# The last output tile cut into 384 and 128 columns, its last part copied and stored by ScalarE

## Chip, cores, metric

One core of one Trainium2 chip. The metric is the device time of one execution in microseconds (us), lower is better.

Names in the profile: PE is TensorE, PEld its weight loads, DVE VectorE, ACT ScalarE, POOL GpSimd, SP SyncE. A "q" after the name is the engine's queue, in which DMAs are issued. L637 is line 637 of the kernel file. A store has "landed" when the last of its 16 completion increments (the counts that its DMA adds to a semaphore) has arrived.

## The reference

Windowed attention with a few global keys (4 batches, 8 heads, 768 positions, head size 64), followed by a feed-forward layer with squared ReLU. Only the last product matters here:

```python
def _moe_ref(x, w_in, w_out):          # x: 3072 x 512, d_ff = 2048
    h = np.maximum(x @ w_in, 0.0)
    return (h * h @ w_out).astype(np.float32)
```

The output is 3072 x 512 in float32, written in 24 tiles of 128 rows. The change concerns the 24th.

## The kernel before

A small planner in Python places operations in an order at build time. An operation is listed with the engines that may do it and their costs. An ordinary output tile is one group of 16 matmuls of 512 columns, one copy out of PSUM and one store of 256 KB. The very last tile has its own function:

```python
    def copy(e, out, in_):
        if e == "ACT":
            nc.scalar.copy(out=out, in_=in_)
        else:
            eng(e).tensor_copy(out=out, in_=in_)
    # ... cut ...
    def last_layer2(x, j):
        n = d_model // 2
        r0 = x.hb * HALF + j * P
        for c in range(0, d_model, n):
            st = {}

            def emit(e, c=c, st=st):
                st["ps"] = bank([P, 512], FP32, "yps")
                for m in range(NFT):                       # NFT = 16
                    nc.tensor.matmul(st["ps"][:, 0:n], lhsT=x.h2[:, m, j * P:(j + 1) * P],
                                     rhs=w_out_sb[:, m, c:c + n], start=m == 0, stop=m == NFT - 1)

            def evac(e, st=st):
                st["y"] = y_p.tile([P, d_model], FP32, name="y", tag="y")
                copy(e, st["y"][:, 0:n], st["ps"][:, 0:n])
            job = plan.pe(NFT * (n / 2400 + 0.003), emit, [x.h2_ops[m, j] for m in range(NFT)], 1)
            y_op = plan.after(job, {"ACT": 0.3, "DVE": 0.35}, evac)
            plan.add({"SP": 0.6}, lambda e, c=c, st=st: nc.sync.dma_start(
                out=out[r0:r0 + P, c:c + n], in_=st["y"][:, 0:n]), [y_op])
    # ... cut ...
        if hb == NHB - 1:
            main = main[:-NFT // 4] + [lambda: last_layer2(x, HT - 1)]
```

So the last tile is already cut in two halves: the copy and the store of the first half go on beside the matmuls of the second.

The softmax here doesn't subtract the row's maximum and nothing guards it: scores larger than these inputs give would overflow.

## Time and profile before

| | before |
|---|---|
| time, median (lowest to highest) | 213.84 us (213.76 to 214.04) |
| span of the profiled execution | 212.0 us |
| TensorE busy | 206.4 us, 97% |
| first matmul of the last tile | 205.22 us |
| last matmul ends | 208.87 us |
| last copy, ScalarE, 256 columns | 208.91 to 209.28 us |
| last store issued, landed | 209.31, 211.0 us |

How to read it: everything up to 208.9 us is bound by TensorE. What can be gained by the change lies in the 3.1 us after it, in which one copy, one store and the closing of the program follow each other with nothing beside them. I call this stretch, from the end of the last matmul to the end of the span, the **tail**. The views that show it stand in the prediction below.

### The profile page before, as it was taken

To read this page: it belongs to the slowest core of one execution; us is meant where nothing else is said; L and a number is where in the kernel's file an instruction comes from. 1 tells how busy PE (TensorE), PEld (TensorE's weight loads), DVE (VectorE), ACT (ScalarE), POOL (GpSimd) and SP (SyncE) were. 2 spreads that over 40 slices of the span, in tenths; PEclk is the share of its full clock that TensorE was granted. 3 is DMA by queue.
4 is the path that set the end of the run, shared out by engine and by line. 5 is a ranking of instruction groups with operands and counts; after the bars stand their busy time and mean duration, and the time that the engine had idled before them with its cause. 6 is when DMAs were issued, how large, how long until landed. Compare 5 with 4: busy or idle time off the path is not lost.

```text
span 212.0 us, 4795 instructions
## 1 busy us (share of the span) xinstructions
PE 206.4 (97%) x1902; PEld 127.6 (60%) x1902; DVE 116.3 (55%) x332; ACT 122.5 (58%) x252; POOL 66.5 (31%) x82
## 2 busy tenths in 40 slices
PE   6999999999999999999999999999999999999994
PEld 7877898755554665456644665456644665455553
DVE  8679878434681678319860778218860777114300
ACT  6899897735741994148811994248811994247421
POOL 8997343594001930094008600095000000000000
PEclk9999999999999999999999999999999999999999
DMA  6999999999954999599988995399941100320012
GB/s 175 167 164 197 199 198 209 163 154 169 179 162 136 118 152 145 136 121 178 142 112 128 168 152 111 91 125 174 153 120 77 53 19 19 90 99 2 0 53 99
DMA packets 106343, 27.06 MB, mean 128 GB/s; under 512 B 96976, under 2 KB 103376, under 8 KB 106320
## 3 DMA queue, kind: packets, MB, share of 16 engines
q0 software_dynamic: 74944, 13.11, 80.0%
q1 hardware_dynamic: 30320, 13.11, 27.4%
q10 hardware_dynamic: 1056, 0.52, 0.8%
q8 instruction: 15, 0.25, 0.5%
q14 instruction: 8, 0.07, 0.1%
HBM read 27.26 MB, written 6.29 MB: 158 GB/s over the span
## 4 chain that ended last, share of the span: by engine, by line
PE 88%; POOL 6%; DMA 5%; DVE 0%; ACT 0%; issue 0%; POOLq 0%
PE hps L560 39%; PE yps L609 38%; DMA w_in_sb<-in_moe_w_in_dram 5%; PE sp L464 4%; PE av L519 4%; POOL v L312 2%; POOL sk L312 2%; POOL sq L312 2%; PE yps L637 2%; PE trp L411 1%; PE av L760 1%; POOL w_in_sb L369 0%; PE trx L787 0%; PE sp L721 0%; DVE ident L239 0%; ACT y L200 0%
## 5 line engine op out<-in xcount | busy, mean ns | idle before, releaser
L560 PE MATMUL hps<-xt,w_in_sb 128*128 128x384 f16 (+2 forms) x608 | 88.0, 301 | 0.1
L609 PE MATMUL yps<-w_out_sb,h 128*128 128x512 f16 x368 | 83.0, 379 | 0.0
L560 PEld LDWEIGHTS <-w_in_sb 128*128 128x128 f16 x608 | 53.9, 98 | 26.9 <-DMA w_in_sb<-in_moe_w_in_dram 0.4
L584 ACT ACTIVATE hr<-hps 128x384 f16<-128x384 f32 (+1 forms) x107 | 55.3, 525 | 13.8 <-PE hps L560 12.0
L609 PEld LDWEIGHTS <-h 128*128 128x128 f16 x368 | 34.9, 98 | 39.0
L200 ACT COPY y<-yps 128x512 f32<-128x512 f32 (+1 forms) x25 | 14.2, 568 | 66.5 <-PE yps L609 56.8
L595 DVE TENSOR_TENSOR h<-hr 128x768 f16<-128x768 f16 (+1 forms) x70 | 35.4, 521 | 24.5 <-ACT hr L584 24.0
L312 POOL DMA_DIRECT2D sq<-in_q_dram x22 | 19.5, 897 | 67.1 <-DMA xt<-tm 63.9
L477 ACT ACTIVATE ex<-sp 128x512 f16<-128x512 f32 x66 | 35.1, 624 | 1.2 <-PE sp L464 1.2
L586 DVE TENSOR_SCALAR hr<-hps 128x384 f16<-128x384 f32 x15 | 8.3, 554 | 38.7 <-PE hps L560 38.7
L312 POOL DMA_DIRECT2D v<-in_v_dram x24 | 21.5, 927 | 4.7 <-DMA w_out_sb<-in_moe_w_out_dram 3.7
L497 DVE TENSOR_TENSOR phat<-ex,mask 128x1024 f16<-128x1024 f16 (+1 forms) x36 | 20.3, 598 | 2.1 <-ACT ex L477 2.1
L312 POOL DMA_DIRECT2D sk<-in_k_dram x22 | 19.5, 910 | 3.4 <-DMA w_out_sb<-in_moe_w_out_dram 2.9
L529 DVE TENSOR_TENSOR tm<-av,rec 128x384 f16<-128x384 f32 x24 | 13.4, 558 | 0.8
L202 DVE COPY vb<-v 128x520 f16<-128x520 f16 (+1 forms) x32 | 10.2, 318 | 3.2 <-DMA v<-in_v_dram 2.7
L519 PEld LDWEIGHTS <-phat 128*128 128x128 f16 x240 | 9.8, 98 | 3.1
L519 PE MATMUL av<-v,phat 128*128 128x65 f16 x144 | 10.9, 194 | 0.0
L519 PE MATMUL av<-vb,phat 128*128 128x65 f16 x96 | 10.1, 194 | 0.0
L464 PEld LDWEIGHTS <-qk 64*128 64x128 f16 x168 | 6.3, 94 | 4.6 <-issue 3.7
L464 PE MATMUL sp<-qk 64*128 64x128 f16 x168 | 8.8, 218 | 0.0
L202 DVE COPY kb<-qk 128x96 f16<-128x96 f16 (+4 forms) x56 | 7.9, 205 | 0.8 <-ACT qk L200 0.4
L527 DVE RECIPROCAL rec<-av 128x6 f32<-128x6 f32 x24 | 4.7, 195 | 6.7 <-PE av L519 6.2
(66 smaller groups left out, 137.8 us busy)
## 6 DMA issues: line engine op xcount, KB each, us to landing
out_dram<-y SPq DMA_DIRECT2D x23, 256.0 KB, 2.2
v<-in_v_dram POOLq DMA_DIRECT2D x24, 128.0 KB, 7.0
sq<-in_q_dram POOLq DMA_DIRECT2D x22, 128.0 KB, 5.7
sk<-in_k_dram POOLq DMA_DIRECT2D x22, 128.0 KB, 6.3
w_in_sb<-in_moe_w_in_dram POOLq DMA_DIRECT2D x4, 512.0 KB, 10.5
w_out_sb<-in_moe_w_out_dram POOLq DMA_DIRECT2D x4, 512.0 KB, 15.7
y<-in_k_dram ACTq DMA_DIRECT2D x2, 256.0 KB, 4.5
y<-in_q_dram SPq DMA_DIRECT2D x2, 256.0 KB, 4.0
```

The costliest lines, as they stand in the source:

```text
L200: nc.scalar.copy(out=out, in_=in_)
L202: eng(e).tensor_copy(out=out, in_=in_)
L312: dma = nc.gpsimd.dma_start(out=dst, in_=src[x.b, :, r0 + t * P:r0 + (t + 1) * P, :] .rearrange("h p d -> p h d"))
L464: nc.tensor.matmul(sp[h][:, i, :], lhsT=lhsT, rhs=bt.qk[rows, 0, r, a, :], start=True, stop=True)
L477: nc.scalar.activation(out=st["ex"][:, h], in_=sp[h], func=AF.Exp, scale=scale)
L497: eng(e).tensor_tensor(out=x.phat[a][:, :, t0:t0 + n], op=ALU.mult, in0=st["ex"][:, :, i0:i0 + 2 * n].rearrange("p e (t b) c -> p e t (b c ...
L519: nc.tensor.matmul(av[:, h, j, :], lhsT=lhsT, rhs=rhs, start=not before, stop=before or r == 0)
L529: nc.vector.tensor_tensor(out=st["tm"].rearrange("p t e d -> p e t d"), in0=av[:, :, :, 0:D], in1=rec[:, :, :, None].to_broadcast([P, 2, H ...
L560: nc.tensor.matmul(st["ps"][:, i * n:(i + 1) * n], lhsT=w_in_sb[:, kk, m * P:(m + 1) * P], rhs=x.xt[:, kk, c0:c1], start=kk == 0, stop=kk ...
L584: nc.scalar.activation(out=o, in_=i, func=AF.Relu)
L595: eng(e).tensor_tensor(out=x.h2[:, m0:m0 + width, c0:c1], in0=hr, in1=hr, op=ALU.mult)
L609: nc.tensor.matmul(st["ps"], lhsT=x.h2[:, m, j * P:(j + 1) * P], rhs=w_out_sb[:, m, :], start=m == 0, stop=m == NFT - 1)
```

## The change

Its intent: a shorter last part (128 columns in place of 256) makes the last copy and the last store shorter. The longer first part is moved out by VectorE, and the last store is issued by ScalarE right behind its own copy, from a queue that holds nothing else.

```diff
-        n = d_model // 2
         r0 = x.hb * HALF + j * P
-        for c in range(0, d_model, n):
+        for c, n in ((0, 384), (384, d_model - 384)):
             st = {}
 ... (n=n, queue=queue handed to the inner functions) ...
-            y_op = plan.after(job, {"ACT": 0.3, "DVE": 0.35}, evac)
-            plan.add({"SP": 0.6}, lambda e, c=c, st=st: nc.sync.dma_start(
+            y_op = plan.after(job, {"DVE" if c == 0 else "ACT": 0.09 + n * 0.001}, evac)
+            q, queue = ("SP", nc.sync) if c == 0 else ("ACT", nc.scalar)
+            plan.add({q: 0.6}, lambda e, c=c, n=n, st=st, queue=queue: queue.dma_start(
                 out=out[r0:r0 + P, c:c + n], in_=st["y"][:, 0:n]), [y_op])
```

More of the change, by code (lines that the diff above doesn't have):

```diff
@@ L628, in last_layer2, with emit @@
     def last_layer2(x, j):
-        n = d_model // 2
         r0 = x.hb * HALF + j * P
-        for c in range(0, d_model, n):
+        for c, n in ((0, 384), (384, d_model - 384)):
             st = {}
-            def emit(e, c=c, st=st):
+            def emit(e, c=c, n=n, st=st):
                 st["ps"] = bank([P, 512], FP32, "yps")
@@ L638, in emit, with evac @@
                                      rhs=w_out_sb[:, m, c:c + n], start=m == 0, stop=m == NFT - 1)
-            def evac(e, st=st):
+            def evac(e, n=n, st=st):
                 st["y"] = y_p.tile([P, d_model], FP32, name="y", tag="y")
```

## The prediction

> **What bounds the kernel now.** I read the busy shares first, then the chain that ended last, then the last seven microseconds in order of time, and last the movement of the final store in quarter microseconds. The page gives a span of 212.0 us and says who is full:
>
> ```profile
> PE 206.4 (97%) x1902; PEld 127.6 (60%) x1902; DVE 116.3 (55%) x332; ACT 122.5 (58%) x252; POOL 66.5 (31%) x82
> ```
>
> TensorE is busy for 97% of the span, so the body is bound by matmuls, and the change does not touch the body. The chain of waits from 195 us on shows where its reach begins:
>
> ```profile
> 198.47 6.91 PE yps L609 x32
> 205.38 3.51 PE yps L637 x32
> 208.89 0.02 issue
> 208.91 0.37 ACT y L200
> ```
>
> Line 637 is the last tile: 32 matmuls of 256 columns, then one copy. Until 208.89 us only matmuls stand on the chain. What follows is an exposed tail of 212.0 - 208.9 = 3.1 us. The timeline of the last stretch, and the source view of the store (for its issue: least, median and largest ns):
>
> ```profile
> 205.22 3.66 PE L637 MATMUL yps<-w_out_sb,h 128*128 128x256 f16 x32
> 205.42 0.59 ACT L200 COPY y<-yps 128x512 f32<-128x512 f32 x1 [2.87 <-PE yps L609]
> 207.16 0.37 ACT L200 COPY y<-yps 128x256 f32<-128x256 f32 x1 [1.16 <-PE yps L637]
> 207.56 2.08 SPq L645 DMA_DIRECT2D out_dram<-y  x2
> 208.91 0.37 ACT L200 COPY y<-yps 128x256 f32<-128x256 f32 x1 [1.38 <-PE yps L637]
> ```
>
> ```profile
> L645 SPq DMA_DIRECT2D out_dram<-y x2: 332/332/332, 207.6 to 209.3; - x2
> DMA to landing us min/median/max: 1.7/1.7/1.7
> ```
>
> The merged store row holds two issues: the first from 207.56, and the last, which ends at 207.56 + 2.08 = 209.64 and so begins at 209.64 - 0.33 = 209.31, some 30 ns after the copy's end at 208.91 + 0.37 = 209.28. It lands at 209.31 + 1.7 = 211.01. The remaining 1.0 us is the closing exchange of semaphores between the engines. The SP queue was idle from 207.89 to 209.31: the second store waited for its copy and not for a busy queue. The window view (length, busy time by engine, then clock, DMA share, GB/s) splits the 1.7 us:
>
> ```profile
> 210.00:210.25 0.25, 0.00 (x0) 0.00 (x0) 0.00 (x0) 0.00 (x0) 0.00 (x0) 1.00 0.34 123
> 210.25:210.50 0.25, 0.00 (x0) 0.00 (x0) 0.00 (x0) 0.00 (x0) 0.00 (x0) 1.00 1.02 361
> 210.50:210.75 0.25, 0.00 (x0) 0.00 (x0) 0.00 (x0) 0.00 (x0) 0.00 (x0) 1.00 0.14 41
> ```
>
> The 16 DMA engines are busy for 0.25 x (0.34 + 1.02 + 0.14) = 0.375 us, from about 210.17 to 210.54. So of the 1.7 us, 0.86 pass from issue to first byte, 0.37 are movement, and 0.47 pass until the completion is seen. The two stores before agree: the one of 207.56 began to move at about 208.42, also 0.86 later, and the 256 KB one of 205.99 moved for 0.68 us and landed in 2.0.
>
> **What the Trainium skill says.** (1) "DMA: Bandwidth & Descriptors", section "Issuing engines are not separate DMA queues": stores issued from ScalarE and from SyncE run on the same 16 DMA engines, and a second issuer only saves sequencer time. The trace gives that saving nothing to take here, the SP queue being idle for 1.4 us. (2) "ScalarE: Activation LUTs", section "What ACT_TABLE_LOAD costs": 0.833 ns per element. The trace agrees: copies of 512 and of 256 columns take 585 and 372 ns, (585 - 372)/256 = 0.832. (3) "TensorE: Matmul & The Clock Gate", section "Back-to-back issue gap": alone N/2.4 + 2.5 ns, but about 81 ns for N = 128 in a stream with weight loads. The 256-column tile agrees with the first form: (3.66 - 0.272)/31 = 109 ns, against 109.2. At 128 columns the trace contradicts the 81 ns, as shown below.
>
> **The change part by part.** In the built instruction streams the two kernels differ only in this last tile: matmuls of 16 x 384 and 16 x 128 columns for 32 x 256, one copy on VectorE and one on ScalarE for two on ScalarE, one store on each queue for two on SP. Nothing earlier moves.
>
> TensorE. Columns and instruction count are unchanged, 16 x 512 and 32. The rates come from a 128-column group in the opening, one of 16 back to back, and from layer 1 near the end of the chain, 64 matmuls of 384 columns:
>
> ```profile
> 19.31 1.06 PE L560 MATMUL hps<-xt,w_in_sb 128*128 128x128 f16 x16
> ```
>
> ```profile
> 188.07 10.40 PE hps L560 x64
> ```
>
> At 128 columns a single matmul shows 219 ns, so the gap is (1.06 - 0.219)/15 = 56 ns; at 384 it is 10.40/64 = 162.5 ns. From 205.22: 16 x 0.1625 = 2.60, the first part's last result at 205.22 + 15 x 0.1625 + 0.326 = 207.98 (326 ns is the mean of 384-column matmuls late in the trace), and the end at 205.22 + 2.60 + 15 x 0.056 + 0.219 = 208.88. Before: 205.22 + 3.66 = 208.88. Gain zero.
>
> First part. VectorE has been idle since 199.6 us, when its last square ended. The nearest row for its copy:
>
> ```profile
> L586 DVE TENSOR_SCALAR hr<-hps 128x384 f16<-128x384 f32 x15 | 8.3, 554 | 38.7 <-PE hps L560 38.7
> ```
>
> So about 208.01 to 208.56, store issued at 208.59. Its 192 KB should move for 0.53 us (halfway between 0.375 for 128 KB and 0.68 for 256), from 209.45 to 209.98, and land near 210.45. It is off the path.
>
> Last part. The copy of 128 columns: 372 - 128 x 0.832 = 265 ns, so 208.91 to 209.175: **0.107 us saved**. Movement: 128 packets of 512 B. The loads on ScalarE's queue at the start give a price for that size, and show what ScalarE's issue costs:
>
> ```profile
> q10 hardware_dynamic: 1056, 0.52, 0.8%
> ```
>
> ```profile
> L357 ACTq DMA_DIRECT2D y<-in_k_dram x2: 482/541/600, 0.7 to 1.2; - x2
> L357 SPq DMA_DIRECT2D y<-in_q_dram x2: 460/472/483, 0.7 to 1.3; - x2
> ```
>
> 0.8% of 16 x 212 us over 1056 packets is 26 ns each; 8 packets per engine make 0.21 us. The line through 128 and 256 KB gives 0.375 - 0.15 = 0.22. So movement falls from 0.375 to 0.22: **0.155 us saved**. First byte and completion stay at 0.86 and 0.47 by assumption. The issue on ScalarE: in the opening the two queues issued side by side, ScalarE's 541 - 472 = 69 ns the slower; late and alone SP needs 332 ns. I put **0.05 us lost** for issue and waking. Sum: 0.107 + 0.155 - 0.05 = 0.21 us. The last store would be issued at about 209.2 to 209.25, land near 210.8 instead of 211.01, and the span become 211.8. With 213.84 us before: 213.63, which I round to 213.62.
>
> **The rivals.** First, ScalarE's queue is the slower issuer, and the gift is taken back: its decode of the store behind its own copy, or its first byte, costs 0.2 us more than SP's. For it, the opening, where its two loads landed in 4.5 us against 4.0 (medians); against it, those four loads competed with each other. The time would be 213.75 to 213.9. Second, the two stores collide. The first part's bytes should leave the engines at 209.98, the last part's arrive at about 210.08: a margin of only 0.1 us. A VectorE copy 0.1 us longer, or a first byte earlier on ScalarE, makes the last store queue behind the first. The loss is bounded by the overlap; I see up to 0.15 us, so 213.65 to 213.75. Third, 128-column matmuls with weight loads run at the 81 ns of the skill: 15 x 25 ns = 0.38 us longer, and the time would be 214.0. The opening group at 56 ns speaks against it. Fourth, for a larger gain: ScalarE, needing no message from another engine, issues at once and receipts of a 64 KB write come quicker; then 0.3 to 0.35 us and 213.5.
>
> **Range and chances.** The whole exposed tail is 3.1 us or 1.5% of the time, of which the change can reach the 0.37 of the copy and part of the 1.7 of the store. No rival moves the result by more than 0.4 us; 2% would be 4.3 us. The runs before spread over 0.28 us, about as much as the gain, so the range is set by noise as much as by the rivals: 213.3 to 213.9. Faster by over 2%: 0.005; within 2%: 0.985; slower by over 2%: 0.01.
>
> **What would show it.** Right: the last matmul still ends within 0.05 us of 208.9; VectorE's copy lies near 208.0 to 208.6; the last ScalarE copy takes 265 ns; its store is issued under 0.1 us after that and lands in about 1.55 us; DMA is busy twice, for 0.53 and for 0.22 us, barely apart; SP still closes 1.0 us after the landing. Wrong: an issue of over 0.45 us or a first byte over 1.0 us after it (first rival); one unbroken stretch of DMA at full share up to the end (second); a 128-column part longer than 1.1 us (third). If the first part landed last, the ordering of the whole argument would have failed.

## The result, and the profile after

| | before | after |
|---|---|---|
| time, median (lowest to highest), 4 runs each | 213.84 (213.76 to 214.04) | 213.62 (213.51 to 213.72) |
| ratio after/before | | 0.9988, 95% interval 0.9971 to 1.0005 |
| span of the profiled execution | 212.0 | 211.8 |
| tail | 3.097 | 2.924 |

Ratios are the mean time of one kernel's fast runs over that of the other's in the same rounds, so they are not quite the ratio of the medians quoted. The two sets of runs don't overlap, but the interval just includes 1. A difference of 0.1% is at the edge of what run times can tell, so the traces carry the argument. The tail is taken from the start and end times of the records, to the nanosecond.

The end of the kernel after, in order of time (start, length, engine, line, operation; in brackets how long the engine had been idle and what ended that):

```profile
205.26 3.66 PE L636 MATMUL yps<-w_out_sb,h 128*128 128x384 f16 x32
205.46 0.59 ACT L200 COPY y<-yps 128x512 f32<-128x512 f32 x1 [2.87 <-PE yps L609]
208.06 0.56 DVE L202 COPY y<-yps 128x384 f32<-128x384 f32 x1 [8.42 <-PE yps L636]
208.64 0.33 SPq L645 DMA_DIRECT2D out_dram<-y  x1
208.95 0.27 ACT L200 COPY y<-yps 128x128 f32<-128x128 f32 x1 [2.91 <-PE yps L636]
209.25 0.37 ACTq L645 DMA_DIRECT2D out_dram<-y  x1
```

The matmul group (the row merges both widths) is 3.66 us long as before. The last copy is 0.27 us in place of 0.37. Its store is issued at 209.25, 30 ns after the copy's end; before it was 209.31, although this execution had entered the last tile 0.04 us later. The source view of the stores:

```profile
L645 SPq DMA_DIRECT2D out_dram<-y x1: 332/332/332, 208.6 to 208.6; - x1
L645 ACTq DMA_DIRECT2D out_dram<-y x1: 367/367/367, 209.2 to 209.2; - x1
DMA to landing us min/median/max: 1.6/1.7/1.8
```

ScalarE's issue is 35 ns longer than SP's; the store of 64 KB lands in 1.6 us where 128 KB took 1.7. And the quarter microseconds of the end (the last two columns are the DMA engines' busy share, which passes 1 where packet records overlap, and GB/s):

```profile
209.50:209.75 0.25, 0.00 (x0) 0.00 (x0) 0.00 (x0) 0.00 (x0) 0.00 (x0) 1.00 0.97 369
209.75:210.00 0.25, 0.00 (x0) 0.00 (x0) 0.00 (x0) 0.00 (x0) 0.00 (x0) 1.00 0.97 363
210.00:210.25 0.25, 0.00 (x0) 0.00 (x0) 0.00 (x0) 0.00 (x0) 0.00 (x0) 1.00 0.37 113
210.25:210.50 0.25, 0.00 (x0) 0.00 (x0) 0.00 (x0) 0.00 (x0) 0.00 (x0) 1.00 0.59 168
```

The first store fills the engines until about 210.1, then the last one moves. In the records the last store's first packet starts 25 ns after the last data packet of the first store has ended. The two do not overlap, but only just.

### The profile page after: what moved, and what is told of

Its sections match the earlier page's. It is cut to its first block, busy times and chain, and to the rows that moved or that the text cites. A ratio compares the mean times of both kernels' runs of the same rounds, so it can differ in the third digit from the quotient of the medians.

```text
span 211.8 us, 4795 instructions
## 1 busy us (share of the span) xinstructions
PE 205.4 (97%) x1902; PEld 125.6 (59%) x1902; DVE 116.2 (55%) x333; ACT 122.0 (58%) x251; POOL 66.7 (31%) x82
## 4 chain that ended last, share of the span: by engine, by line
PE 90%; DVE 3%; POOL 3%; DMA 3%; issue 0%; ACT 0%; POOLq 0%
PE hps L560 40%; PE yps L609 38%; PE sp L464 4%; PE av L519 4%; DMA v<-in_v_dram 3%; PE yps L636 2%; DVE tm L772 1%; POOL sq L312 1%; POOL v L312 1%; POOL sk L312 1%; PE av L760 1%; PE trx L787 1%; PE trp L411 1%; DVE vb L202 1%; PE sp L721 0%; DVE ph L742 0%
```

## The experiments

Two theories stood at the start. **A**: the sizes carry the whole gain; ScalarE's queue gives nothing and costs about 0.05 us. **B**: the free queue of ScalarE carries it. Later came **C**: the two stores crowd each other on the DMA engines when the first part is late; and **D**: a free queue is worth something only where two issues come close to each other.

All edits are in the list of parts of the last tile. To keep them short, a diff shows this list as (first column, columns, engine of the copy, queue of the store); the changed kernel is `(0, 384, DVE, SP), (384, 128, ACT, ACT)`. All results were correct. The table has the runs in order of the argument. The first three figures are counted in us from the end of the last matmul, from the trace records; "last byte" is the end of the last data packet.

| kernel | last store issued | last byte | tail | median us | before, same chip | ratio (95%) |
|---|---|---|---|---|---|---|
| before | 0.434 | 1.758 | 3.097 | 213.84 | | |
| after | 0.333 | 1.568 | 2.924 | 213.62 | 213.84 | 0.9988 (0.9971 to 1.0005) |
| after_again | 0.333 | 1.569 | 2.921 | 213.51 | 213.86 | 0.9986 (0.9973 to 0.9998) |
| cut_only | 0.328 | 1.500 | 2.867 | 213.56 | 213.86 | 0.9986 (0.9973 to 0.9998) |
| cut_only_again | 0.328 | 1.498 | 2.889 | 213.48 | 213.73 | 0.9989 (0.9976 to 1.0003) |
| queue_only | 0.439 | 1.800 | 3.142 | 213.87 | 213.86 | 0.9999 (0.9986 to 1.0013) |
| last_on_sp | 0.327 | 1.520 | 2.868 | 213.58 | 213.86 | 0.9988 (0.9976 to 1.0001) |
| whole | 0.649 | 2.274 | 3.669 | 214.25 | 213.82 | 1.0019 (1.0003 to 1.0034) |
| cut320 | 0.383 | 1.629 | 2.950 | 213.65 | 213.82 | 0.9990 (0.9976 to 1.0003) |
| cut448 | 0.281 | 1.892 | 3.370 | 214.07 | 213.82 | 1.0010 (0.9997 to 1.0024) |
| cut448_sp | 0.648 | 1.892 | 3.358 | 214.17 | 213.73 | 1.0018 (1.0004 to 1.0031) |
| three | 0.383 | 1.533 | 2.800 | 213.55 | 213.82 | 0.9987 (0.9975 to 1.0000) |
| three_act | 0.279 | 1.433 | 2.682 | 213.45 | 213.73 | 0.9987 (0.9974 to 0.9999) |

A word on noise. The last tile begins at 205.04 to 205.38 us in these profiles although nothing before it differs, a spread of 0.34 us. The tail of a kernel profiled twice repeats to 0.003 us (after) and 0.022 us (cut_only), its last byte to 0.002 us in both. Other kernels were profiled once. So differences under 0.1 us are read from the tails, and the times only confirm the direction of the larger ones.

### after_again: the measure

No edit.

> The changed kernel once more, as the measure for the other runs of this chip. Both theories: 0.20 us (0.15 to 0.3) under the kernel before; last store issued on ScalarE about 30 ns after its copy, issue 367 ns, landing 1.6 us after it.

Measured: tail 2.921 us, issue 366 ns, landing 1.6 us after it. In time it is 0.35 us under the kernel before, more than expected; its profiled execution entered the last tile at 205.17, 0.09 us earlier than the first one, which may be part of it and is no merit of the change.

### cut_only: the sizes alone

```diff
-(0, 384, DVE, SP), (384, 128, ACT, ACT)
+(0, 384, ACT, SP), (384, 128, ACT, SP)
```

> Cut 384 and 128, both copies on ScalarE, both stores on SP. Theory A (the sizes carry the whole gain: a copy shorter by 0.106 us and a store that moves shorter by about 0.15; ScalarE's queue gives nothing and costs some 0.05): 0.25 us under the kernel before, 0.05 under the changed one; last store issue 332 ns, landing in 1.55 us. Theory B (the gain needs the free queue of ScalarE): 0.1 us or less under the kernel before.

The end of cut_only in order of time:

```profile
205.28 3.66 PE L636 MATMUL yps<-w_out_sb,h 128*128 128x384 f16 x32
...
208.09 0.48 ACT L200 COPY y<-yps 128x384 f32<-128x384 f32 x1 [2.01 <-PE yps L636]
208.59 1.01 SPq L645 DMA_DIRECT2D out_dram<-y  x2
208.98 0.27 ACT L200 COPY y<-yps 128x128 f32<-128x128 f32 x1 [0.41 <-PE yps L636]
```

ScalarE is done with the first part 0.41 us before it is needed for the last one, so VectorE was not needed. The SP row holds two issues, the second from 208.59 + 1.01 - 0.33 = 209.27 on, 25 ns after the copy by the records. The tail is 2.867 us (2.889 in the repeat): the whole gain and 0.04 to 0.06 us more, on SP alone. Theory B has fallen as far as the size goes: without ScalarE's queue, 0.30 us in time against the 0.1 or less that B allowed, and again 0.25 in the repeat.

### queue_only: the queue alone

```diff
-(0, 384, DVE, SP), (384, 128, ACT, ACT)
+(0, 256, ACT, SP), (256, 256, ACT, ACT)
```

> Cut 256 and 256 as before, both copies on ScalarE, only the last store moved to ScalarE's queue. Theory A: 0.05 us slower than the kernel before; issue 367 ns in place of 332 and first byte 0.90 us after it in place of 0.84. Theory B: faster by 0.1 us or more.

```profile
209.05 0.37 ACT L200 COPY y<-yps 128x256 f32<-128x256 f32 x1 [1.38 <-PE yps L636]
209.45 0.37 ACTq L645 DMA_DIRECT2D out_dram<-y  x1
```

The store goes out 30 ns after the copy, as on SP, so no waking time is saved. The issue takes 366 ns for 332, the first byte comes 0.87 us after its start (0.90 expected), the last byte is 0.042 us later, and the tail is 3.142 us, 0.045 longer than before. In time nothing moves (ratio 0.9999). B is refuted from this side too; A's 0.05 us holds in the tail, and the times are too coarse to show it.

### last_on_sp: the queue undone

```diff
-(0, 384, DVE, SP), (384, 128, ACT, ACT)
+(0, 384, DVE, SP), (384, 128, ACT, SP)
```

> The changed kernel with its last store back on SP (copies on VectorE and ScalarE stay). Theory A: 0.05 us under the changed kernel, the same as cut_only. Theory B: 0.15 us or more over the changed kernel. Theory C (the two stores crowd each other on the 16 DMA engines): no gain against the changed kernel, for the last store's bytes would come 0.05 us earlier and meet the end of the first store's.

Tail 2.868 us, 0.055 under the changed kernel and the same as cut_only, as A said. The medians say the opposite by 0.07 us (213.58 to 213.51 for after_again), which is within the spread of the starts of the tile (205.28 here, 205.17 there) and far from the 0.15 that B asked for. C shows only faintly: with the same issue time as in cut_only the last byte came 0.02 us later, because VectorE's copy ends 0.08 us after ScalarE's would and the first store's bytes are still leaving. The tail shows no cost.

### whole and cut320: the dose

```diff
-(0, 384, DVE, SP), (384, 128, ACT, ACT)
+(0, 512, ACT, SP)                              # whole
+(0, 320, DVE, SP), (320, 192, ACT, SP)         # cut320
```

> The last tile not cut at all: one copy of 512 columns on ScalarE, one store of 256 KB on SP. Theory A (from the end of the last matmul the tail is the last copy, 159 ns + 0.832 ns per column, plus the last store's movement, some 0.08 us + 0.3 us per 128 KB, plus a fixed rest): copy 0.21 us and store 0.30 us longer than before, less 0.04 us for 16 fewer matmuls: tail about 3.6 us against 3.10, time 0.45 us over the kernel before. A rival by which a part's size hardly matters (the fixed delays hide it): within 0.1 us of it.

> Cut 320 and 192, first copy on VectorE, last on ScalarE, both stores on SP. Theory A: between the kernel before and last_on_sp: last copy 319 ns, tail about 2.98 us from the end of the last matmul (3.10 before, 2.87 for a last part of 128 columns), time 0.12 us under the kernel before. A rival with a step and not a slope (the gain comes from VectorE or from a store of 64 KB or less): tail 2.87 or 3.10.

The last copy and the last store of whole:

```profile
208.87 0.59 ACT L200 COPY y<-yps 128x512 f32<-128x512 f32 x1 [2.87 <-PE yps L636]
209.48 0.33 SPq L645 DMA_DIRECT2D out_dram<-y  x1
```

Tail 3.669 us (expected 3.6) and time 0.43 us over the kernel before (expected 0.45). The last copy of cut320 took 320 ns and its tail was 2.950 us (expected 2.98); its time was 0.17 us under the kernel before (expected 0.12). With the stores on SP the tails form a slope and not a step: 3.669, 3.097, 2.950, 2.867 us for last parts of 512, 256, 192 and 128 columns. From 256 to 128 columns that is 0.23 us, what the cut in two gave without the queue. Counted to the last byte the slope is straight: 2.274, 1.758, 1.629 and 1.500 us, or 0.129 us for every 64 columns. The tail adds to it what follows the last byte, which is taken apart further below.

### cut448 and cut448_sp: too far

```diff
-(0, 384, DVE, SP), (384, 128, ACT, ACT)
+(0, 448, DVE, SP), (448, 64, ACT, ACT)         # cut448
+(0, 448, DVE, SP), (448, 64, ACT, SP)          # cut448_sp
```

> The changed kernel with its cut at 448 and 64. Theory C (the stores crowd each other when the first part comes late): the first copy ends some 0.05 us before the last one, its 224 KB are in the engines' way from 1.05 to 1.67 us after the last matmul, the last store's bytes end behind or among them: tail 3.0 to 3.15 us, as long as before although the last part is half as long. Rival (only the last part's size counts): last copy 212 ns, tail 2.80 us, 0.1 us under the changed kernel.

cut448 in order of time, then its quarter microseconds:

```profile
208.51 0.62 DVE L202 COPY y<-yps 128x448 f32<-128x448 f32 x1 [8.85 <-PE yps L636]
208.97 0.21 ACT L200 COPY y<-yps 128x64 f32<-128x64 f32 x1 [2.91 <-PE yps L636]
209.16 0.33 SPq L645 DMA_DIRECT2D out_dram<-y  x1
209.22 0.37 ACTq L645 DMA_DIRECT2D out_dram<-y  x1
```

```profile
210.00:210.25 0.25, 0.00 (x0) 0.00 (x0) 0.00 (x0) 0.00 (x0) 0.00 (x0) 1.00 0.95 373
210.25:210.50 0.25, 0.00 (x0) 0.00 (x0) 0.00 (x0) 0.00 (x0) 0.00 (x0) 1.00 1.04 401
210.50:210.75 0.25, 0.00 (x0) 0.00 (x0) 0.00 (x0) 0.00 (x0) 0.00 (x0) 1.00 0.94 256
```

The two copies end within 0.05 us of each other and the stores are issued 0.06 us apart, each from a queue of its own. DMA is then full in one stretch: 224 KB and 32 KB go one behind the other. The last store's first packet starts 1.34 us after its issue, in place of 0.90, and 5 ns after the start of the first store's earliest completion write. The Trainium skill, "DMA: Bandwidth & Descriptors", section "Queues, rings and completion order", says that an engine drains a whole packet of some 9 to 17 descriptors from one queue before it turns to another. The trace agrees: a store has 128 data records and 16 completions, so 8 and 1 for each engine, and no record of the second store stands before the first store's earliest completion write has started. Simple order of arrival would look the same.

C is right in kind and was too mild in size: tail 3.370 us, expected 3.0 to 3.15. The first store left the engines at 1.773 us in place of 1.67, the last byte came at 1.892, and what follows the last byte took 1.48 us, against 1.25 to 1.40 in the kernels not cut at 448. This last 0.1 us appears in both kernels cut at 448. The traces place it: the last completion increment came 0.51 and 0.50 us after the last byte, against 0.35 to 0.41 elsewhere, and the closing after it was no longer than before. Why the increment came later stays open.

> Cut at 448 and 64, both stores on SP. With the last store on ScalarE the tail was 3.37 us: its first byte came 1.34 us after its issue, when the first store left the first DMA engine. Theory C (the DMA engines are the wait, each serving the first store whole before the second): SP must issue the second some 0.3 us later and it does not matter, tail 3.30 to 3.40. Rival (two queues in flight at once are what costs): tail 3.0 to 3.2.

With one queue SP could issue the second store only at 0.648 us, 0.37 later than ScalarE did, and the tail was 3.358 us, no longer. So two queues were not what cost, and they gained nothing: the wait was at the DMA engines. The rival, 3.0 to 3.2, has fallen.

### three and three_act: three parts

```diff
-(0, 384, DVE, SP), (384, 128, ACT, ACT)
+(0, 256, ACT, SP), (256, 192, DVE, SP), (448, 64, ACT, SP)     # three
+(0, 256, ACT, SP), (256, 192, DVE, SP), (448, 64, ACT, ACT)    # three_act
```

> Three parts of 256, 192 and 64 columns: copies on ScalarE, VectorE, ScalarE, all stores on SP. Theory A: nothing crowds the last store; last copy 212 ns; tail 2.75 us; 16 more matmuls cost 0.04 us; 0.08 us under cut_only, 0.33 under the kernel before. Rival: packets of 256 B cost as much as those of 512 B: tail 2.82, no gain over cut_only.

Its end in order of time:

```profile
205.38 3.70 PE L636 MATMUL yps<-w_out_sb,h 128*128 128x256 f16 x48
...
207.72 2.12 SPq L645 DMA_DIRECT2D out_dram<-y  x3
208.65 0.36 DVE L202 COPY y<-yps 128x192 f32<-128x192 f32 x1 [8.89 <-PE yps L636]
209.11 0.21 ACT L200 COPY y<-yps 128x64 f32<-128x64 f32 x1 [1.41 <-PE yps L636]
```

The matmuls took 0.04 us longer, as worked out. The tail was 2.800 us, shorter by 0.07 than cut_only but not the 2.75 expected. Even this 0.07 is not the smaller part's merit: the last completion increment arrived 1.897 us after the last matmul in both, and only the closing was shorter, 0.90 us for 0.97. The copy ended at 209.32, yet SP issued the third store only at 207.72 + 2.12 - 0.39 = 209.45: its second issue stood in the way. The rival has the wrong cause: packets of 256 B took 17.6 ns on average, those of 512 B 26.8. Two issues on SP could not follow each other faster than 0.425 us, here as in cut448_sp. This is the one place where a free queue could be worth something, which made theory D:

> Three parts of 256, 192 and 64 columns with the last store on ScalarE's queue. In the run with all three stores on SP the last store was issued 0.13 us after its copy's end and took 391 ns, for SP was still issuing the second. Theory D (here, and only where two issues come closer than some 0.4 us, a free queue is worth something): issue 30 ns after the copy, 367 ns, first byte 0.9 us after that, tail 2.74 to 2.77 us against 2.80 with SP. Rival: the bytes of the second store, up to 1.16 us after the last matmul, hold the last store back anyway: tail 2.80 or more.

```profile
205.30 3.70 PE L636 MATMUL yps<-w_out_sb,h 128*128 128x256 f16 x48
...
208.57 0.36 DVE L202 COPY y<-yps 128x192 f32<-128x192 f32 x1 [8.89 <-PE yps L636]
209.03 0.21 ACT L200 COPY y<-yps 128x64 f32<-128x64 f32 x1 [1.41 <-PE yps L636]
209.27 0.37 ACTq L645 DMA_DIRECT2D out_dram<-y  x1
```

The issue follows its copy by 30 ns again and the tail is 2.682 us, 0.12 under three and more than D had asked for. The 0.12 lies in the last byte, at 1.433 for 1.533, and in the stretch after it, 1.25 us for 1.27. Against cut_only, 0.11 us of the shorter tail come before the last increment and 0.07 from the closing, as in three. Counted from the first matmul of the last tile, three_act needs 3.696 + 2.682 = 6.38 us, cut_only 6.52, the changed kernel 6.58, the kernel before 6.75.

> 384 and 128 with both copies on ScalarE and both stores on SP, again, beside three_act on one chip: tail 2.87 us and 0.25 to 0.3 us under the kernel before; three_act 0.05 to 0.08 us under this one.

On one chip three_act took 213.45 us and cut_only_again 213.48, where 0.05 to 0.08 was expected. The ratios to the kernel before, 0.9987 and 0.9989, cannot be told apart. three_act is the shortest by its trace, and no time here proves it faster than cut_only or the changed kernel; it, the changed kernel (in after_again) and cut_only (in its first runs) are faster than the kernel before, by 0.13 to 0.14%, with intervals that just exclude 1.

## Why the prediction was right

- **Bound and reach.** Right. The chain was matmuls until 208.9 us, and only the 3.1 us behind them could move. No version of the last tile moved the time by more than 0.2%.
- **TensorE, gain zero.** Right: 3.657 us before, 3.656 after. The third rival, 81 ns for a matmul of 128 columns, did not appear: in the last tile after the change they start 55 to 56 ns apart.
- **The last copy, 0.107 us.** Right: 372 to 266 ns.
- **Movement, 0.155 us.** Right in size with the queue held fixed: from issue to last byte 1.758 - 0.434 = 1.324 us before and 1.500 - 0.328 = 1.172 in cut_only, 0.152 less. The split was misread, though: I had 0.86 us to the first byte, 0.37 of movement and 0.47 to the completion; in the records it is 0.835, 0.489 (first to last byte) and 0.355. The difference of two stores hides this. My sign "lands in about 1.55 us" did not come either: 1.63.
- **The queue, 0.05 us lost.** Right, and tested from both sides: the tail grew by 0.045 when the queue was changed alone, and shrank by 0.055 when it was undone. Hardly any of it is waking time (30 ns after the copy, 26 on SP). In both pairs 0.034 to 0.035 us of it is the longer issue; the other 0.01 to 0.02 is spread over the waits before and after. The first rival, a loss of 0.2 us, was right in sign only; the fourth, a gain from the own queue, was wrong.
- **The sum.** 0.21 us was predicted; the tail shrank by 3.097 - 2.924 = 0.173. In its terms: 0.101 until the issue; 0.089 from issue to last byte, which is 0.151 for the movement less 0.035 for ScalarE's issue and 0.027 for a first packet that came later after the issue's end; and 0.017 lost after the last byte, a term that I had taken as constant (0.040 lost until the last increment, 0.023 won in the closing). The medians differ by 0.22. That this is so near to the prediction is partly luck, since the start of the last tile wanders by more than the 0.04 in question.
- **Collision, the second rival.** I gave the two stores a margin of 0.1 us. It was 0.025. The step that failed is "should move for 0.53 us": that is the mean busy time of an engine, but the 16 engines start and end one after another, and the first store moved from 0.563 to 1.205 us, 0.64 long. At 384 columns it cost little: at most the 0.027 and the 0.040 of the sum above, and no run shows that these come from the first store. At 448 it cost 0.45 us against the changed kernel, three times the 0.15 that I had set as the most for a collision (at 384): with a first part that late the last store waits for the whole of the first, not for an overlap.

The stretch after the last byte, 1.25 to 1.48 us, falls into two parts in the traces. Until the last completion increment it took 0.35 to 0.36 us in the kernels before, queue_only, whole, cut320, three and three_act, 0.39 to 0.41 where 64 KB came right behind 192 KB, and 0.50 to 0.51 where 32 KB came right behind 224 KB. So it did not follow the last store's own size; why it grew behind a large store stays open. The closing after it took 1.04 us with one part (whole), 0.96 to 0.99 with two and 0.90 with three. SyncE waits there for the semaphores of the DMAs in a fixed order, some 60 ns a step, and with each further store the last one's semaphore stood one step later, so that fewer steps were left. A comparison of tails between one, two and three parts has this in it.

## What to carry to other kernels

When the body is bound by one engine, try cutting the last tile unevenly: here the last part set the tail through its copy and its store, and halving its 256 columns gave 0.23 us, 0.1% of the time. Place the cut so that the bytes of the part before are out of the DMA engines when the last part's come, counting the time from first to last byte and not the mean busy time: at 448 columns a smaller last part cost more than the old halves did; no cut between 384 and 448 was tried. A second issuing queue paid only where the last two issues came closer than one queue allows (0.425 us here) and the DMA engines were free in time (three_act); at 448 it gained nothing, and elsewhere it cost 0.05 us.

## What the Trainium skill lacked or had wrong

- "DMA: Bandwidth & Descriptors" gives no difference between the issuers SP and ACT. Here an issue alone took 332 ns on SP and 366 to 367 on ACT, and moving the last store to ACT lengthened the tail by 0.045 to 0.055 us. Nor does it give a time for how close two issues on one queue can follow: 0.425 us here.
- The same page gives about 0.6 us to the first byte for these queues and does not say from when. From the start of the issue it was 0.83 us on SP (whole) and 0.87 to 0.90 on ACT; from its end 0.50 to 0.52 us on SP and 0.51 to 0.53 on ACT, but for the two kernels cut at 448.
- It has no time from the last data byte to the last completion increment on these queues: 0.35 to 0.36 us here, up to 0.51 right behind a larger store.
- "TensorE: Matmul & The Clock Gate" gives about 81 ns per matmul at 128 columns in a stream with weight loads. Here the gap was 56 ns, in the opening and in the last tile, and a last tile with 16 such matmuls was as long as one without, 3.656 to 3.657 us. The form that the prediction quotes for a matmul alone held in the stream at every width that was run: 29 ns at 64 columns, 82 to 83 at 192, 109 at 256, 136 at 320, 162 to 163 at 384, 189 to 190 at 448, 215 to 216 at 512.
